# A 27th seven-product unit and one written order for the whole stream: attention and a gated feed-forward block on one core

## The chip, the core and the metric

The kernel runs on one core of a Trainium2 chip. The metric is the device time of one execution in microseconds. Before the change the median of three runs was 404.07 us (403.4 to 404.55).

The core has a matrix engine (TensorE, PE in the profile), whose loads of stationary weights are listed apart (PEld); VectorE (DVE), ScalarE (ACT) and GpSimd (POOL) for elementwise work; and SyncE (SP), which only issues transfers here. POOL issues the loads, SP the transposing transfers and the stores, ACT a few stores at the end. Each engine runs its own instructions in the order in which the program gave them, and waits for the others by semaphores.

## The reference

```python
def _attn_ref(q, k, v):                       # q, k, v: (8, 12, 448, 64)
    scores = scale * np.matmul(q, k.transpose(0, 1, 3, 2))
    attn = np.maximum(scores, 0.0) ** 2 / S
    return np.matmul(attn, v)
...
def _moe_ref(x, w_gate, w_val, w_out):        # x: (3584, 768), d_ff = 1536
    g = x @ w_gate
    gelu = 0.5 * g * (1.0 + erf(g * inv_sqrt2))
    val = x @ w_val
    return gelu * val @ w_out
```

There are eight batches of 12 heads with 448 positions. Attention squares the positive part of the scores in place of a softmax, so no sum over a row is needed. Its output, with the heads side by side, is the input of the feed-forward block.

## The kernel before

**Tiles of the matrix engine.** Nearly every matmul uses one quarter of the array: 64 rows by 64 columns, chosen by a row half and a column half. `mm` (line 364) issues it; this is the line 365 under which nearly all matmuls appear. Two matmuls of the two column halves go out together, and two streams, called PE0 and PE1 in the planner, feed the two row halves side by side.

**Batches.** A batch goes through these steps:
- Loads of q, k and v by POOL (`load_qk`, `load_v`).
- Transposes of q and k: on the matrix engine for batches 0 and 1 (`add_transposes`, an item "t"), by a DVE copy and two transposing transfers on SP's queue for later batches (`add_dma_transposes`, copy at line 475, transfers at line 480).
- 21 scores items (`add_scores`, an item "s"): four matmuls, a relu on ACT (line 714) and a square on DVE (line 728).
- Six values items (`add_values`, "v"), each for a pair of heads, and a scaled copy into `xT` (line 792).
- Gate and value: the 1536 columns of each of the two weights lie in 12 blocks of 128. A plain item (`add_gate_value`) makes one block of gate or of value for a batch with 24 matmuls of 448 columns; a gelu on ACT (line 1044) reads the gate, a multiplication on DVE (line 1049) the value.
- Down products: `add_product`, by groups of four chunks of 64 tokens, seven products of 24 matmuls with 384 columns in place of eight, their sums at line 1143, the results read at lines 1223 and 1225, stored at line 1241.

**Seven-product units.** `add_pair` makes gate and value of two neighbouring blocks at once, as one seven-product scheme of 2 by 2 blocks: the tokens of a batch are cut into two halves of 224 (`halves`), the inner dimension into two halves of 384. Each of the products, named 1 to 7, has 24 matmuls of 224 columns. Three results are copied by ACT (line 962), three are added by DVE (line 966), two gelus (line 970) and two multiplications (line 975) follow. The scheme needs sums of the weights, four for each pair of blocks (`add_pair_sums`, line 870, an item "w"), and sums of the tokens, four for each batch (`add_token_sums`, line 894). `NPB` says how many units a batch has: (0, 1, 2, 3, 4, 4, 6, 6), 26 in all. The other blocks are plain.

**Order.** `LINE` lists gate and value items (a digit is the batch), products of units ("3B6" is batch 3, second unit, product 6) and down products ("d4" is the fourth group, product 4). Before the change, transposes, scores and values are not in `LINE`: lines 1335 to 1376 work out a place for each from the start of the batches in `LINE` and from the twelve numbers of `SHIFT`, and the weight sums are put behind the last plain item of the batch ahead of their first use. `START` is the order of batch 0's attention.

**Planner.** What is placed up to `FIXED` is a fixed list (batch 0's attention, the first transposes of batch 1, the first two plain items). Everything later is a `Unit`. `run_plan` keeps a time for each engine by given costs, and when the matrix engine is free and the fixed list is used up, `next_unit` looks at the first 40 units (`AHEAD`) by rank and takes the first that is ready, or the earliest. Scores may also be put into the midst of another unit. The emitted program is what the planner chose; on the chip each engine's order is then fixed.

**Banks.** The PSUM has two double banks for scores at first. `next_scores` gives one of them up at a point that is called `WIDE` (20.0 on the planner's scale), for two more banks for the feed-forward block; from there each scores item waits for the relu of the one before.

The lines on which the argument rests:

```python
    NPB = (0, 1, 2, 3, 4, 4, 6, 6)
...
        if at > WIDE and n % SB == 0 or wide:
...
    for b, m in late:
        add_dma_transposes(b, m)
```

Of the kernel before, what the change touches and what calls it, by code (L numbers as in the profile page):

```python
# [11 lines left out]
LINE = """  # L12
0 0 0 0 0 0 0 0 0 0 0 0 0 0 0 0 0 0 0 0 0 0 0 0 1 1A1 1 2 1A6 2 2 1 1A7 1A2 1A5 2 a1 2 a2 2A1 1A4 1
1 1 1A3 1 2 1 2A2 a6 1 2A7 a7 2 1 a5 1 1 2A6 2 2 1 1 1 1 a3 1 1 a4 1 1 b1 b7 c1 b2 b6 2A4 2 c6 b4 b5
c7 c5 2B1 2B6 c4 2B2 c3 b3 2A5 2 c2 2B7 2B4 2B5 2A3 2 3A1 2 3A2 2 2B3 2 2 3A6 3A7 d7 d1 3B1 d2 4C1
3B2 3 3C1 3B7 3 d6 3 e1 d4 3C7 3 3C6 3 3B6 e7 3B4 e6 3A4 3A5 3 3 3 3C2 3 3B5 3 3 d5 3C4 3A3 3C5 d3
4A1 4C2 3B3 3C3 e5 3 4A7 f1 f2 f6 e4 f7 4C7 4 e2 4C6 4A2 e3 g7 4B1 f5 4B6 4 4A6 4B2 g1 4B7 4 g2 4A5
4C5 4A4 4B4 4B5 f4 4D7 4D1 4C4 4 5B1 5 4D6 4D5 4A3 4 g6 4 g5 4C3 4B3 f3 4 5 5B2 4D2 4D4 g3 4D3 5C1
g4 5B6 5B7 5C2 5B5 5A1 4 5A6 5 5C7 5A7 5A2 5 5B4 5D1 h1 5A4 5D6 5D2 h6 5C6 h7 5 5D7 5D5 5A5 6A1 5B3
5 5C5 5C4 5A3 5C3 5D4 6B1 5 5D3 5 6A2 6B2 h4 i1 i2 6B7 6A6 i7 h5 6A7 h2 6D1 6F7 6D7 h3 j1 6D6 6C1  # L20
6D2 i6 j7 6E1 j6 6C7 6C2 6E7 i5 i4 6C6 6B6 6A5 6A4 6E6 6A3 6F1 6B4 6B5 6C5 6D5 6D4 6F6 i3 6B3 6F5
6C4 j5 6D3 6E2 6F2 6E5 6F4 6C3 6F3 6E4 6E3 7E7 j2 7E1 7B1 k1 k7 7E2 7A1 7B2 7B7 k2 7B6 7E6 j4 7C1 k6
7A2 l7 7C7 7C6 7A7 7B4 7C2 l1 7B5 7B3 k5 7A6 7F1 j3 7D1 7E5 7F7 7F2 7A5 k4 7F6 7E4 l6 7D7 7C4 7D2
7F4 7D6 7D5 7D4 7D3 l2 7F5 7A4 7C5 7C3 7E3 7A3 l5 l4 7F3 m1 n1 m7 k3 l3 m2 m6 n6 m5 n7 n4 m3 n5 n2
m4 n3
# [7 lines left out]


SHIFT = "-183 -79.5 40.75 1.75 -343.75 -112 43.75 -179.5 27.25 -513.5 -447.25 0.25"
# [60 lines left out]
class Unit:  # L96


    def __init__(self, at, los, his, box=None, closer=None, prev=None):
        self.at, self.los, self.his, self.box, self.closer, self.prev = at, los, his, box, closer, prev  # L100
        self.begun = False
        self.short = False
# [3 lines left out]
BANK = 0.3  # L106


def run_plan(queues, pools, units, banks, arrivals, together, fill, blocks, span):
# [48 lines left out]
    def next_unit(short):  # L158
        best = None
        now = max(free["PE0"], floor)  # L160
        for u in units[:AHEAD]:
# [16 lines left out]
            if u.box is not None:  # L178
                k, end = None, None
                for n, c in banks.items():  # L180
                    x = 0.0 if c is None else c.end
                    if x is not None and (end is None or x < end):
                        k, end = n, x
                if k is None:
                    continue
                t = max(t, end + BANK)
            if short and t > now:
                continue
            t = max(t, now)
            if best is None or t < best[0]:  # L190
                best = (t, u, k)
# [7 lines left out]
    while left:  # L199
# [33 lines left out]
        if isinstance(op, tuple):  # L233
            _, u, k = op
            u.begun = True
            units.remove(u)
            if k is not None:
                u.box["k"] = k
                banks[k] = u.closer()
            queues["PE0"][at["PE0"]:at["PE0"]] = u.los  # L240
# [36 lines left out]
def kernel(  # L277
# [39 lines left out]
    NPB = (0, 1, 2, 3, 4, 4, 6, 6)  # L317
    ROOM = 4
    RING_V, RING_T, RING_H, RING_R, RING_A, RING_O = 3, 3, 2, 2, 4, 4
    SINGLE = "3"  # L320
    RING_M, RING_G = 5, 4
# [17 lines left out]
    loaded = tc.tile_pool(name="lpool", bufs=2), tc.tile_pool(name="hpool", bufs=RING_H)  # L339
# [126 lines left out]
    def add_dma_transposes(b, m, deps=()):  # L466
# [23 lines left out]
        copy = Op("DVE", 0.62, emit_copy, [wait, *(regrouped[n - 2] if n > 1 else ())], lag=0.15, prio=1)  # L490
# [43 lines left out]
    def next_scores(at):  # L534

        n = len(units)
        if at > WIDE and n % SB == 0 or wide:
# [48 lines left out]
    def then(at, step, los, his, box=None, closer=None):  # L586

        if not isinstance(at, list) and at > FIXED:
# [3 lines left out]
            later.append(Unit(at, los, his, box, closer))  # L592
# [567 lines left out]
    def add_product(at, gr, name, final):  # L1160
# [103 lines left out]
        then(at, RS, *ops, box if name in opens else None, lambda: st["read", stages_last[stage]])  # L1264
# [38 lines left out]

    work = []
    flow = [[("g", b, fc, g) for fc in range(2 * NPB[b], FC) for g in range(2)] for b in range(B)]
    line = []
    for x in LINE.split():
        if len(x) == 1:
            line.append(flow[int(x)].pop(0))
        elif len(x) == 3:  # L1310
            line.append(("7", int(x[0]), "ABCDEFGHIJKL".index(x[1]), x[2]))
        else:
            line.append(("p", "abcdefghijklmn".index(x[0]), x[1]))
    assert not any(flow)
    at = 0.0
    starts = [None] * B
    placed = []
    for item in line:
        if item[0] == "g" and starts[item[1]] is None:
            starts[item[1]] = at  # L1320
        if item[0] == "7" and starts[item[1]] is None:
            starts[item[1]] = at
        placed.append((at, item))
        at += {"g": G, "7": G / 2, "p": R}[item[0]]
    starts.append(at)
    WIDE = 20.0
    for at, item in placed:
        if item[0] == "g":
            work.append((at, 5, add_gate_value, item[1:]))
        elif item[0] == "7":  # L1330
            work.append((at, 5, add_pair, item[1:]))
        else:
            _, gr, name = item
            work.append((at, 5, add_product, (gr, name, gr == B * SC // 4 - 1)))
    LEAD = 6.0

    LO1 = 2.0
    for b in range(B):
        if b == 0:
            lo, hi = -60.0, -12.0  # L1340
        elif b == 1:
            lo, hi = LO1, starts[1] - LEAD
# [154 lines left out]
```

## Time and profile before

| | us |
|---|---|
| median of the runs | 404.07 |
| span of the profiled execution, first to last instruction | 394.9 |
| median less that span | 9.2 |
| PE busy | 386.3 |
| DVE busy | 309.6 |
| ACT busy | 258.7 |
| POOL busy | 97.2 |
| mean granted clock of TensorE, share | 0.998 |

The page has the busy time of each engine, the span in slices, the chain of work that ended last, and the costliest groups of instructions, each with its count, its busy time, the mean of one in ns, and the idle time of the engine ahead of it with what ended that. Times of instructions that overlap are counted once in a busy time. The profiled execution's own time is not listed apart from its span.

Further views that are used: a table of stretches (busy time of each engine in a stretch, the number of instructions in brackets, the granted clock, the share of the transfer engines and GB/s), the timeline (start, length, engine, line, operation, and in square brackets the idle time before it with its releaser), and the groups with different shapes kept apart.

### The profile page before, as it was taken

What the parts mean: (1) busy time and instruction counts of PE and PEld (TensorE: products, weight loads), DVE (VectorE), ACT (ScalarE), POOL (GpSimd) and SP (SyncE); (2) the same over time, 40 slices, a digit from 0 to 9 for tenths busy, and PEclk for the clock granted to TensorE, in tenths of its full rate; (3) what the DMA queues carried; (4) which work ended last, traced back from release to release, by engine and by line L of the source; (5) the groups of instructions that cost most, each with busy time, mean ns of one, the idle gap of its engine ahead of it and who ended that gap; (6) DMA issues with size and microseconds to landing.
All of it is one profiled execution on the core that took longest, in us unless ns stands there. A gap on an engine that the chain in (4) does not pass through costs nothing.

```text
span 394.9 us, 22904 instructions
## 1 busy us (share of the span) xinstructions
PE 386.3 (98%) x10570; PEld 358.4 (91%) x10573; DVE 309.6 (78%) x522; ACT 258.7 (66%) x401; POOL 97.2 (25%) x156
## 2 busy tenths in 40 slices
PE   7999999999999999999999999999999999999995
PEld 3458889999999999999999999989999999999994
DVE  3885779968797499999797779758988999866772
ACT  5866872357677767787786478765787886535541
POOL 7656523322233323232332123310211000000000
PEclk9999999999999999999999999999999999999999
DMA  8999999988999969887999598880763501121134
GB/s 110 186 199 199 197 209 185 112 103 83 161 148 175 152 85 143 93 132 121 113 148 108 124 122 111 139 83 11 103 105 56 125 6 43 45 45 45 43 85 120
DMA packets 85567, 45.12 MB, mean 114 GB/s; under 512 B 46048, under 2 KB 82400, under 8 KB 85472
## 3 DMA queue, kind: packets, MB, share of 16 engines
q0 software_dynamic: 46944, 24.39, 49.9%
q1 hardware_dynamic: 37888, 18.49, 26.4%
q8 instruction: 82, 1.34, 1.4%
q10 hardware_dynamic: 640, 0.79, 0.6%
q14 instruction: 13, 0.11, 0.1%
HBM read 48.76 MB, written 11.01 MB: 151 GB/s over the span
## 4 chain that ended last, share of the span: by engine, by line
PE 93%; DVE 2%; DMA 2%; POOL 1%; issue 1%; ACT 0%; ACTq 0%; POOLq 0%
PE ff L365 85%; PE sp L365 7%; DMA qk<-in_k_dram 2%; DVE attnT L728 1%; PE sp L646 1%; POOL qk L424 1%; DVE xT L792 0%; PE ff L646 0%; ACTq L1241 0%; ACT osb L1225 0%; ACT rl L714 0%; PE ff L567 0%; DVE osb L1223 0%; DVE qkT L650 0%; POOL ident masks.py:199 0%
## 5 line engine op out<-in xcount | busy, mean ns | idle before, releaser
L714 ACT ACTIVATE rl<-sp 128x896 bf16<-128x896 f32 x168 | 152.1, 919 | 50.4 <-PE sp L365 45.1
L365 PE MATMUL ff<-xT,wg 64*64 64x224 bf16 (+1 forms) x2304 | 183.7, 299 | 0.6 <-issue 0.6
L365 PEld LDWEIGHTS <-wv 64*64 64x64 bf16 x2304 | 127.7, 107 | 4.4
L365 PEld LDWEIGHTS <-wg 64*64 64x64 bf16 x2304 | 123.3, 107 | 5.0 <-issue 0.5
L365 PE MATMUL ff<-xT,wv 64*64 64x448 bf16 x1056 | 120.8, 349 | 0.0
L728 DVE TENSOR_TENSOR attnT<-rl 128x1792 bf16<-128x1792 bf16 (+1 forms) x98 | 92.2, 952 | 6.6 <-ACT rl L714 6.2
L365 PEld LDWEIGHTS <-ws 64*64 64x64 bf16 x1872 | 92.3, 107 | 1.4 <-issue 1.0
L365 PEld LDWEIGHTS <-s 64*64 64x64 bf16 x1344 | 81.6, 107 | 1.8
L365 PE MATMUL ff<-attnT,v 64*64 64x448 bf16 (+1 forms) x768 | 79.7, 326 | 0.7 <-DVE attnT L728 0.6
L365 PE MATMUL ff<-ts,wv 64*64 64x224 bf16 x1248 | 78.7, 256 | 0.0
L365 PE MATMUL ff<-ts,ws 64*64 64x224 bf16 x1248 | 77.6, 256 | 0.0
L365 PE MATMUL sp<-qkT 64*64 64x448 bf16 (+1 forms) x768 | 74.6, 328 | 0.7 <-issue 0.3
L365 PE MATMUL ff<-wo,s 64*64 64x384 bf16 x672 | 63.4, 323 | 0.0
L966 DVE TENSOR_TENSOR part<-ff,part 128x448 f32<-128x448 f32 x78 | 47.5, 622 | 20.1 <-PE ff L365 16.4
L365 PEld LDWEIGHTS <-uT 64*64 64x64 bf16 x1008 | 62.5, 107 | 0.7
L365 PE MATMUL ff<-wt,s 64*64 64x384 bf16 x672 | 61.4, 322 | 0.0
L365 PE MATMUL ff<-wo,uT 64*64 64x384 bf16 x672 | 60.7, 322 | 0.0
L962 ACT COPY part<-ff 128x448 f32<-128x448 f32 x78 | 41.3, 534 | 12.4 <-PE ff L365 11.2
L443 POOL DMA_DIRECT2D v<-in_v_dram x48 | 29.6, 620 | 80.3 <-ACT rl L714 44.3
L365 PEld LDWEIGHTS <-v 64*64 64x64 bf16 x768 | 44.7, 107 | 4.1 <-issue 1.7
L424 POOL DMA_DIRECT2D qk<-in_q_dram x43 | 27.6, 642 | 80.0 <-ACT rl L714 59.5
L1049 DVE TENSOR_TENSOR uT<-gel,ff 128x448 bf16<-128x448 bf16 x44 | 27.3, 620 | 22.4 <-PE ff L365 11.0
(51 smaller groups left out, 423.9 us busy)
## 6 DMA issues: line engine op xcount, KB each, us to landing
out_dram<-osb SPq DMA_DIRECT2D x48, 192.0 KB, 3.3
v<-in_v_dram POOLq DMA_DIRECT2D x48, 128.0 KB, 4.1
wg<-in_moe_w_gate_dram POOLq DMA_DIRECT2D x6, 384.0 KB, 10.4
wv<-in_moe_w_val_dram POOLq DMA_DIRECT2D x6, 384.0 KB, 11.0
wo<-in_moe_w_out_dram POOLq DMA_DIRECT2D x4, 576.0 KB, 14.9
qk<-in_q_dram POOLq DMA_DIRECT2D x18, 128.0 KB, 3.5
qk<-in_k_dram POOLq DMA_DIRECT2D x18, 128.0 KB, 4.3
qk<-in_q_dram POOLq DMA_DIRECT2D x18, 96.0 KB, 3.8
```

What stands on the lines that cost most here:

```text
L365: ins = nc.tensor.matmul(o, lhsT, rhs, start=start, stop=stop, skip_group_check=onto, tile_position=(P * row, P * col))
L424: return nc.gpsimd.dma_start(qk16[b, m][HALF[i], r0:r0 + h1 - h0, cols], src[b, h0:h1].rearrange("h (p c) d -> p h (c d)", c=SC)[:, :, cols])
L443: return nc.gpsimd.dma_start(v16[b, m][HALF[i], h0 % 4:h0 % 4 + h1 - h0, :, :], v[b, h0:h1].rearrange("h (p c) d -> p h c d", c=SC)[:, :, ...
L646: blocks.add(nc.tensor.transpose(t[HALF[j], c, :], src[:, 2 * r + j, c, :], ident[:, :], tile_position=(0, P * j)))
L714: relu.ins = nc.scalar.activation(duo["rl"][:, u % 2, :, :], box[0][:, :, 0:S], AF.Relu).ins
L728: nc.vector.tensor_tensor(a[:, part], duo["rl"][:, part], duo["rl"][:, part], op=ALU.mult)
L962: rd.ins = nc.scalar.copy(st["t", name][:, :], box[0][:, 0:S]).ins
L966: rd.ins = nc.vector.tensor_tensor(t[:, :], box[0][:, 0:S], t[:, :], op=ALU.add).ins
L1049: u_op[b, fc].ins = nc.vector.tensor_tensor(uT[b][:, fc, :], gel.pop((b, fc))[:, :], box[0][:, 0:S], op=ALU.mult).ins
```

## The change

- `NPB` is (0, 2, 2, 3, 4, 4, 6, 6): batch 1 has two units, 27 in all.
- `LINE` is replaced by one of 566 items that also holds the scores "s", values "v" and transposes "t" of batches 1 to 7, each in its natural sequence, and the weight sums "w0" to "w5". `SHIFT` and the lines that worked out places are gone; an item's place is 1.0 plus its number in `LINE`.
- `WIDE` is now a count: 44 scores and transposes items.
- `Unit` and `run_plan` learn of a unit that takes a second bank (`more`, `full`, `COVER`), and the ring of `lpool` has a name, `RING_L`.
- The pools of loads are also closed at the end when nothing closed them earlier.

```diff
@@ LINE @@
-0 0 0 0 0 0 0 0 0 0 0 0 0 0 0 0 0 0 0 0 0 0 0 0 1 1A1 1 2 1A6 2 2 1 1A7 1A2 1A5 2 a1 2 a2 2A1 1A4 1
...
-7F4 7D6 7D5 7D4 7D3 l2 7F5 7A4 7C5 7C3 7E3 7A3 l5 l4 7F3 m1 n1 m7 k3 l3 m2 m6 n6 m5 n7 n4 m3 n5 n2
-m4 n3
+s s t s s 0 0 0 v 0 s w0 0 0 s s s v s 0 0 0 t s s s s s s s s v s 0 0 0 v v s s s s s s s s s s s s
+s v 1B1 w1 1B7 1A7 s v 1 1 1 1 0 s s 0 0 0 1A1 s 0 1 1 1 s s s s s s 0 0 s s 1B2 v v 1B6 0 a7 1B5
+1B4 s s 1 1 1B3 1A6 1A5 0 a1 1A2 0 a2 1 1A4 a6 1A3 a5 a4 2A1 1 1 v a3 1 v b1 s s s 1 1 s v 2A2 1 b6
...
+7D6 7A5 7F4 7A4 7F3 7D5 7E3 7D4 k4 7B5 7D3 7C5 7C3 7A3 7B4 7B3 l2 m1 m7 l6 k3 m6 m5 l5 l3 n1 n6 n7
+m4 n5 n3 n4 l4 m3 n2 m2
...
-SHIFT = "-183 -79.5 40.75 1.75 -343.75 -112 43.75 -179.5 27.25 -513.5 -447.25 0.25"
...
+            k2 = None
+            if u.more is not None:
+                for n, c in banks.items():
...
+            if k2 is not None:
+                u.more[0]["k"] = k2
+                banks[k2] = u.more[1]()
+                if not full[k2]:
+                    u.more[0]["cover"] = True
+                    u.los[0].cost += COVER
...
-    NPB = (0, 1, 2, 3, 4, 4, 6, 6)
+    NPB = (0, 2, 2, 3, 4, 4, 6, 6)
...
+    RING_L = 2
...
-        if at > WIDE and n % SB == 0 or wide:
+        if n >= WIDE and n % SB == 0 or wide:
...
+    for x in START.split():
+        at = placed0[x.rstrip("a")]
...
+    work.append((PLACE5, add_values, (0, NPAIR - 1)))
+    work.append((PLACE5 + 0.05, add_transposes, (1, 0, (0, 1))))
+    for g in range(2):
+        work.append((0.0, add_gate_value, flow[0].pop(0)[1:]))
+    for n, x in enumerate(LINE.split()):
+        at = 1.0 + n
+        if x[0] == "w":
+            work.append((0.0, lambda at, i: add_pair_sums(i), (int(x[1]),)))
+        elif x == "s":
+            work.append((at, add_scores, flow_s.pop(0)))
...
+    WIDE = 44
...
+    if not rest:
+        for pool in loaded:
+            pool.__exit__(None, None, None)
```

140 lines of the change are left out of this document (53 added, 87 removed).

## The prediction

> **What bounds the kernel now.** I read the page's first part, then its chain of waits, then a table of stretches.
>
> ```profile
> span 394.9 us, 22904 instructions
> PE 386.3 (98%) x10570; PEld 358.4 (91%) x10573; DVE 309.6 (78%) x522; ACT 258.7 (66%) x401; POOL 97.2 (25%) x156
> ...
> PE 93%; DVE 2%; DMA 2%; POOL 1%; issue 1%; ACT 0%; ACTq 0%; POOLq 0%
> ```
>
> ```profile
> 0.00:10.00 10.00, 7.98 (x78) 3.79 (x79) 3.09 (x8) 5.50 (x8) 7.88 (x18) 1.00 0.82 111
> 10.00:20.00 10.00, 9.08 (x140) 4.90 (x142) 8.25 (x15) 8.35 (x11) 6.01 (x9) 1.00 1.36 186
> 20.00:30.00 10.00, 9.14 (x161) 5.35 (x158) 8.75 (x16) 5.85 (x8) 5.40 (x8) 1.00 1.37 199
> 60.00:70.00 10.00, 10.00 (x232) 9.20 (x228) 9.20 (x18) 2.63 (x5) 2.45 (x4) 1.00 1.24 174
> 70.00:80.00 10.00, 10.00 (x277) 9.68 (x271) 9.59 (x18) 3.17 (x7) 3.93 (x6) 1.00 1.10 120
> 260.00:270.00 10.00, 9.35 (x330) 8.98 (x324) 6.33 (x12) 6.27 (x13) 0.61 (x1) 1.00 0.59 45
> 390.00:394.90 4.90, 0.73 (x10) 0.30 (x5) 0.00 (x0) 0.75 (x2) 0.00 (x0) 0.82 0.50 139
> ```
>
> TensorE is the bound: 93% of the chain. The columns after each stretch are its length and the busy time of PE, weight loads, DVE, ACT and POOL. PE is idle for 394.9 - 386.3 = 8.6 us, and these rows hold it all: 2.02, 0.92 and 0.86 in the first 30 us, 0.65 in 260 to 270, 4.17 at the end. So after the first 30 us there is one visible hole. But "busy" is not "at its pace", so I count the work after 30 us and give it its pace.
>
> ```profile
> L365 PE MATMUL ff<-xT,wv 64*64 64x448 bf16 x1046 | 119.7, 349 | 0.0
> L365 PE MATMUL ff<-xT,wg 64*64 64x448 bf16 x1042 | 117.4, 349 | 0.0
> L365 PE MATMUL ff<-ts,wv 64*64 64x224 bf16 x1248 | 78.7, 256 | 0.0
> L365 PE MATMUL ff<-ts,ws 64*64 64x224 bf16 x1248 | 77.6, 256 | 0.0
> L365 PE MATMUL ff<-xT,wg 64*64 64x224 bf16 x1248 | 76.0, 256 | 0.6 <-issue 0.6
> L365 PE MATMUL ff<-attnT,v 64*64 64x448 bf16 x504 | 65.2, 349 | 0.0
> L365 PE MATMUL ff<-wo,s 64*64 64x384 bf16 x672 | 63.4, 323 | 0.0
> L365 PE MATMUL ff<-wt,s 64*64 64x384 bf16 x672 | 61.4, 322 | 0.0
> L365 PE MATMUL ff<-wo,uT 64*64 64x384 bf16 x672 | 60.7, 322 | 0.0
> L365 PE MATMUL sp<-qkT 64*64 64x448 bf16 x504 | 56.9, 349 | 0.0
> L365 PE MATMUL ff<-xT,ws 64*64 64x224 bf16 x624 | 39.6, 256 | 0.0
> L365 PE MATMUL ff<-wt,uT 64*64 64x384 bf16 x336 | 34.1, 323 | 0.0
> L365 PE MATMUL ff<-attnT,v 64*64 64x224 bf16 x168 | 23.5, 256 | 0.0
> L365 PE MATMUL sp<-qkT 64*64 64x224 bf16 x168 | 9.8, 256 | 0.0
> L646 PE MATMUL sp<-ident,qk 128*64 128x128 bf16 x56 | 2.1, 222 | 0.0
> ```
>
> ```profile
> 259.31 0.35 PE L365 MATMUL ff<-xT,wg 64*64 64x448 bf16 x2
> ...
> 260.07 0.35 PE L365 MATMUL ff<-xT,wg 64*64 64x448 bf16 x2
> ...
> 263.10 0.80 PE L365 MATMUL ff<-ts,wv 64*64 64x224 bf16 x24
> 263.68 0.26 PE L365 MATMUL ff<-ts,ws 64*64 64x224 bf16 x2
> ...
> 266.12 0.25 PE L365 MATMUL ff<-xT,wg 64*64 64x224 bf16 x1 [0.65 <-issue]
> ```
>
> ```profile
> 383.30 0.33 PE L365 MATMUL ff<-wt,uT 64*64 64x384 bf16 x2
> ...
> 384.11 0.33 PE L365 MATMUL ff<-wt,uT 64*64 64x384 bf16 x2
> ...
> 388.35 2.38 PE L365 MATMUL ff<-wo,s 64*64 64x384 bf16 x36
> ```
>
> The first block counts matmuls from 30 us on; the others are the timeline of PE. A 64*64 matmul fills a quarter of the array, so its listed duration (349 ns) is latency and the distance between starts is the price. From 259.31 to 260.07 the pairs of one row half advance four times, 0.19 us each, and the other half runs beside it: four 448-column matmuls cost 0.19 us. The 24 matmuls of 224 columns, which are one of the seven products, take 263.68 - 263.10 = 0.58 us. Five steps from 383.30 to 384.11 make 0.162 us for four of 384 columns.
>
> Demand after 30 us: 448 columns, 1046 + 1042 + 504 + 504 = 3096, by four, by 0.19: 147.1. Columns 224: 3 x 1248 + 624 + 168 + 168 = 4704, by 24, by 0.58: 113.7. Columns 384: 3 x 672 + 336 = 2352, by four, by 0.162: 95.3. The transposes 2.1. Together 358.2 us. The last matmul ends at 388.35 + 2.38 = 390.73, so 360.7 us were there: **2.5 us** is all that the order of the work loses after 30 us. (A pace is read to about 0.5%, so this is good to 2 us.) Of it 0.65 is the hole before 266.12. About 0.6 belongs to the end: the last 36 matmuls start over 2.38 - 0.32 = 2.06 us, where their pace would be 36 / 4 x 0.162 = 1.46, since the second row half of a last product runs alone. That stays with any order. So **1.9 us** can be won by order.
>
> **The change part by part.**
>
> The unit. Batch 1 has two blocks of gate and value that took four plain products of 24 matmuls with 448 columns: 4 x 6 x 0.19 = 4.56 us. The second unit takes seven products: 7 x 0.58 = 4.06. It saves **0.50 us**. All of it counts, since PE sets the end.
>
> On the rows above, 24 ns pass for each matmul of 224 columns. [...]
>
> What the unit adds on other engines:
>
> ```profile
> L966 DVE TENSOR_TENSOR part<-ff,part 128x448 f32<-128x448 f32 x78 | 47.5, 622 | 20.1 <-PE ff L365 16.4 <-ACT part L962 3.1
> L962 ACT COPY part<-ff 128x448 f32<-128x448 f32 x78 | 41.3, 534 | 12.4 <-PE ff L365 11.2 <-DVE uT L975 0.3
> L870 DVE TENSOR_TENSOR ws<-ws,wg 128x768 bf16<-128x768 bf16 x6 | 3.3, 552 | 0.0
> L1223 DVE TENSOR_TENSOR osb<-ff,osb 128x384 f32<-128x384 f32 x42 | 23.2, 555 | 8.9 <-PE ff L365 7.5 <-issue 0.5 <-ACT part L962 0.3
> L1225 ACT COPY osb<-ff 128x384 f32<-128x384 f32 x56 | 26.7, 478 | 23.2 <-PE ff L365 22.8
> ```
>
> Three adds of 0.622 on DVE (1.9 us) and three copies of 0.534 on ACT (1.6 us); gelus and multiplications are two and two in both forms. DVE is at 78% and ACT at 66%, so over the whole run they lie beside PE. The four sums of the second weight block (4 x 0.55 = 2.2 us on DVE) were made before too, but now they stand in the list ahead of batch 1's units. That cover is thin from 60 to 80 us, where DVE is at 9.20 and 9.59 of 10; if it is gone, rival D prices it.
>
> The new order. START and what is placed up to FIXED are as before, and later units may start only when that list is used up, about 30 us; so the first 30 us and their 3.8 us of holes stay. I cost them at nothing. From there each item's place in LINE is its rank, and the planner still takes the first ready one of 40, so the list is a preference. It can win at most the 1.9 us, and it can lose: it moves scores, with them the loads that wait for relus, the transposes on SP's queue and the stores behind these. The trace of before can't show where those land. Bounds: -1.9 (every loss gone) and +2.9 (rival D). I take half of what can be won, **-0.95**: the hole at 266.12 is tied to what ran beside it there, and the new list puts other items there, while the thin spread of the rest has no one cause that an order takes away. This is nearer to the lower bound because only one hole is seen in 360 us.
>
> The changed loads, the branch that closes pools, "full", "more" and COVER: no caller gives "more", so no second bank is taken and COVER isn't added. RING_L is the 2 that stood there. WIDE as 44 counts scores and transposes of the first two batches (21 + 21 + 3 = 45), the same place as before within one unit. Nothing for these.
>
> The end. The last item was n3, read by a copy on ACT; now it is m2, read by an add on DVE: 0.555 - 0.478 = **+0.08 us**. The store after it goes by the same two queues.
>
> Sum: -0.50 - 0.95 + 0.08 = -1.4 us. The profiled execution's span is 394.9, so the new span is 393.5; outside it lie 404.07 - 394.9 = 9.2 us to the median of the runs, which I carry over. **Forecast 402.7 us**, -0.34%.
>
> **The rivals.**
>
> B, the order wins all: -0.50 - 1.9 + 0.08 gives 401.7, and with the 2 us of doubt in the pace 399.7 at the far end. For it: scores were placed by a few shifts for each batch and can now stand anywhere. Against: the 1.9 us is spread thin.
>
> C, the order wins nothing: only the unit and the end, 403.6 us. For it: the planner deviates from the list whenever an item isn't ready, in both kernels, so the executed orders may differ little in quality.
>
> D, slower: DVE becomes the bound between 60 and 80 us. Sums of the second weight block (2.2 us) and the three adds (1.9) move in where 0.80 + 0.41 = 1.2 us is free: DVE is 2.9 us late, the products of batch 1 wait for its sums, the first down products after them, and PE with all of them. 404.07 - 0.42 + 2.9 = 406.6 us. It decides as soon as DVE is asked for more than 10 us in 10 while no ready plain unit is left. Against it: ten of batch 0's gate and value units stand behind the second block's sums in the new list and need nothing from them.
>
> E, slower: holes of "issue" like the one at 266.12 multiply.
>
> ```profile
> q8 instruction: 82, 1.34, 1.4%
> DMA to landing us min/median/max: 2.7/4.6/7.2
> ```
>
> The first row counts the packets that bring instructions: 1.34 MB in 82, 16.3 KB each, for 10570 + 10573 PE instructions, or 258 in one. In a stretch of 224-column products one lasts 129 x 24 ns = 3.1 us. The second is the landing time of the 36 transposing transfers (qkT from qkr), 4.6 us: longer than a block lasts, so a block that comes in behind one can be late. The new unit adds 7 x 24 - 4 x 24 = 72 matmuls and as many loads. If the new order puts three more transfers beside such stretches: 3 x 0.65 = +1.95, and 404.07 - 0.42 + 1.95 = 405.6 us. Against it: in 360 us with 36 such transfers it shows once.
>
> [...] That the hole at 266.12 is a late block is my reading; no row names it.
>
> **How the numbers follow.** From no change this kernel can be told at about 0.3%, 1.2 us: faster is below 402.86, slower above 405.28. The forecast has 0.44, and its own range, 401.8 to 403.6, goes over the lower bound: 0.29 faster, 0.15 same. B has 0.17, all faster. C has 0.12, of it 0.02 faster by the doubt in the pace and 0.10 same. D has 0.14 and E 0.13, slower both but for 0.02 of E that stays within the bound. So 0.48 faster, 0.27 same, 0.25 slower. The range goes from B's far end, 399.7, to D's 406.6, and leaves out D's upper half and what is worse.
>
> **What would show it.** Right: 7 x 26 + 7 = 189 products of 24 matmuls, PE busy past 98%, the last matmul some 1.4 us before 390.7; no PE idle above 0.3 us after 30 us. The unit's step is wrong if starts within a seven product are more than 0.58 us apart. D shows as PE idle, or matmuls below pace, between 50 and 100 us with DVE as the releaser; E as "issue" holes beside transposing transfers. The forecast as a whole is wrong if the first 30 us differ, or if scores starve: the relu (L714) then waits longer for PE and the values come late.

## The result: slower by 0.7%, and the profile after

| | before | after |
|---|---|---|
| median of 19 runs each, us | 400.74 (396.91 to 404.55) | 403.13 (399.49 to 406.25) |
| ratio, 95% interval | 1 | 1.007 (1.0047 to 1.0092) |
| time of the profiled execution, us | not listed | 404.35 |
| its span, us | 394.9 | 402.6 |

The ratios, here and below, leave out the few slow runs, so they differ a little from the quotients of the medians.

The forecast was 402.7 us, faster by 0.34%. The change is slower. That 403.13 lies near 402.7 is no merit: the base has moved, since the three runs of 404.07 that the prediction started from stand at the upper end of the 19.

The first parts of the page of after:

```profile
span 402.6 us, 23039 instructions
PE 389.4 (97%) x10642; PEld 356.8 (89%) x10645; DVE 312.0 (78%) x525; ACT 262.9 (65%) x404; POOL 96.5 (24%) x156
...
q8 instruction: 83, 1.36, 1.4%
...
PE 91%; DMA 3%; DVE 2%; issue 2%; ACT 1%; ACTq 0%; POOL 0%; POOLq 0%
```

TensorE is still the bound, and the 72 more matmuls of the second unit are there (10642 - 10570). But PE is now idle for 402.6 - 389.4 = 13.2 us where it was idle for 8.6, and it is busy for 3.1 us more although the unit asks for 0.5 us less. The first number is holes; what the second is comes below. Where the holes are shows in the stretches of 10 us of after (columns as before: length, busy time of PE, weight loads, DVE, ACT, POOL, then clock, share of the transfer engines, GB/s):

```profile
0.00:10.00 10.00, 8.31 (x77) 3.99 (x78) 2.71 (x7) 5.00 (x7) 7.38 (x17) 1.00 0.78 104
10.00:20.00 10.00, 9.63 (x147) 5.14 (x147) 8.70 (x16) 8.93 (x12) 6.53 (x10) 1.00 1.37 191
20.00:30.00 10.00, 9.13 (x156) 5.14 (x156) 8.58 (x16) 5.69 (x7) 6.05 (x10) 1.00 1.37 199
60.00:70.00 10.00, 9.00 (x234) 8.02 (x229) 8.05 (x14) 2.70 (x6) 2.45 (x4) 1.00 1.25 177
130.00:140.00 10.00, 8.51 (x245) 7.71 (x240) 6.51 (x10) 6.65 (x11) 2.61 (x4) 1.00 1.16 192
140.00:150.00 10.00, 8.82 (x243) 8.42 (x235) 6.43 (x10) 6.56 (x10) 2.45 (x4) 1.00 0.56 71
260.00:270.00 10.00, 9.74 (x338) 9.43 (x330) 8.55 (x15) 7.82 (x13) 2.34 (x4) 1.00 0.50 61
```

The first 30 us have 2.93 us of idle PE (3.80 before). From 60 to 70, where before had none, 1.00 us is lost, from 130 to 150 it is 2.67. The hole of before, at 266, is smaller. The table of what PE waited for after 28 us, first before, then after (us in total, times, the longest):

```profile
PE ff L365 <- issue: 0.6, 1, 0.6
```

```profile
PE ff L386 <- issue: 5.0, 11, 1.2
PE sp L386 <- DMA qkT<-qkr: 0.7, 1, 0.7
PE sp L386 <- issue: 0.2, 1, 0.2
```

L386 is the line that was 365. **"Issue" means that PE waited for nothing that the profile shows**: no engine, no bank, no transfer of data. One such hole became twelve, 5.2 us together. Six of them in the timeline of PE (start, length, and in brackets the idle time ahead):

```profile
58.18 0.38 PE L386 MATMUL ff<-xT,wv 64*64 64x448 bf16 x2 [0.16 <-issue]
64.10 0.38 PE L386 MATMUL ff<-xT,wg 64*64 64x448 bf16 x2 [0.37 <-issue]
69.47 0.28 PE L386 MATMUL ff<-ts,ws 64*64 64x224 bf16 x2 [0.62 <-issue]
...
132.10 0.25 PE L386 MATMUL ff<-ts,ws 64*64 64x224 bf16 x1 [0.35 <-issue]
...
138.12 0.28 PE L386 MATMUL ff<-attnT,v 64*64 64x224 bf16 x1 [1.14 <-issue]
...
143.49 0.28 PE L386 MATMUL ff<-ts,wv 64*64 64x224 bf16 x2 [1.18 <-issue]
```

The listed idle time is less than what a hole costs, since it counts from the end of the last matmul, 0.26 to 0.35 us behind its start. From the last start ahead of a hole to the first behind it the twelve come to 8.7 us (0.50 at 58.18, where 0.16 is listed). So the holes also account for most of the busy time that was gained: the other 3.5 us lie under PE's busy time.

And the stretches of after from the end of one hole to the end of the next:

```profile
58.18:64.10 5.92, 5.55 (x128) 4.80 (x128) 4.45 (x8) 2.48 (x5) 1.22 (x2) 1.00 1.23 205
64.10:69.47 5.37, 4.75 (x128) 4.27 (x128) 4.45 (x9) 1.61 (x3) 1.83 (x3) 1.00 1.36 173
132.10:138.12 6.02, 4.88 (x128) 4.30 (x128) 3.68 (x6) 4.48 (x7) 1.72 (x3) 1.00 1.27 212
138.12:143.49 5.37, 4.19 (x128) 3.87 (x128) 4.22 (x7) 2.37 (x3) 1.50 (x3) 1.00 0.93 135
```

This is the reading on which most of what follows rests. Between two neighbouring holes stand exactly 128 matmuls and 128 weight loads, 256 instructions, in each of the four. A packet of instructions holds 1.36 MB / 83 = 16.4 KB, and there are (10642 + 10645) / 83 = 256 matmuls and weight loads for each. So the holes look like late instruction blocks, and the time from one to the next, 5.4 to 6.0 us here, is how long a block took to come.

No row of the page names them so, but the trace has the start and the length of each packet of the instruction queue, q8. The views of the transfers show them too: from 58.18 to 61.80 us there is no packet of q8, and from 61.80 to 62.80 there is this one, whose 6.1% of 16 engines' time in 1 us are 0.97 us:

```profile
q8 instruction: 1, 0.02, 6.1%
```

| hole before ended, us | packet starts | lasts | landed | next hole ends | from landing to that |
|---|---|---|---|---|---|
| 58.18 | 61.82 | 0.97 | 62.79 | 64.10 | 1.31 |
| 64.10 | 67.23 | 0.96 | 68.19 | 69.47 | 1.28 |
| 132.10 | 135.73 | 0.94 | 136.67 | 138.12 | 1.45 |
| 138.12 | 141.09 | 0.97 | 142.06 | 143.49 | 1.43 |

The same holds in all the profiled executions of this document, 20 of them: each of their 84 "issue" holes between 30 and 386 us ends at the same place in its execution's count of 256, within one instruction, and 1.2 to 1.7 us behind the landing of a packet. And in none of the 1611 blocks of these traces does the first instruction start sooner than 1.2 us behind a landing (1.27 in before, 1.22 in after). **So the holes are late instruction blocks.** What is late is the packet's start: it lasts 1.0 us in the median, but starts up to 4.2 us behind the border at which the block ahead of its own begins to run (below, "its border"). In none of them does it start more than 0.3 us before that border (0.24 in before).

128 matmuls of 224 columns are used up in 128 x 24 ns = 3.1 us, 128 of 448 columns in 32 x 0.19 = 6.1 us. From hole to hole above it takes 5.4 to 6.0 us: a block of wide matmuls lasts that long, a block of narrow ones doesn't.

In before the late blocks cost PE 0.6 us of "issue" in 395 us, in after 5.2 us in 403.

### The profile page after: what moved, and what is told of

It is laid out like the page before. It is cut to its first block, busy times and chain, and to the rows that moved or that the text cites. A ratio compares the mean times of both kernels' runs of the same rounds, so it can differ in the third digit from the quotient of the medians.

```text
span 402.6 us, 23039 instructions
## 1 busy us (share of the span) xinstructions
PE 389.4 (97%) x10642; PEld 356.8 (89%) x10645; DVE 312.0 (78%) x525; ACT 262.9 (65%) x404; POOL 96.5 (24%) x156
## 3 DMA queue, kind: packets, MB, share of 16 engines
q8 instruction: 83, 1.36, 1.4%
## 4 chain that ended last, share of the span: by engine, by line
PE 91%; DMA 3%; DVE 2%; issue 2%; ACT 1%; ACTq 0%; POOL 0%; POOLq 0%
PE ff L386 81%; PE sp L386 8%; DMA qkT<-qkr 2%; DVE attnT L749 1%; ACT rl L735 1%; DMA qk<-in_k_dram 1%; PE sp L667 1%; DVE xT L813 0%; PE ff L667 0%; PE ff L588 0%; ACTq L1262 0%; PE ff L630 0%; ACT osb L1246 0%; DVE osb L1244 0%; DVE qkT L671 0%
## 5 line engine op out<-in xcount | busy, mean ns | idle before, releaser
L735 ACT ACTIVATE rl<-sp 128x896 bf16<-128x896 f32 x168 | 151.9, 921 | 51.6 <-PE sp L386 48.0
L386 PE MATMUL ff<-xT,wg 64*64 64x224 bf16 (+1 forms) x2304 | 177.3, 297 | 0.4 <-issue 0.4
L386 PEld LDWEIGHTS <-wv 64*64 64x64 bf16 x2304 | 124.2, 107 | 6.7 <-issue 3.4
L386 PEld LDWEIGHTS <-wg 64*64 64x64 bf16 x2304 | 122.3, 107 | 4.8 <-issue 1.1
L386 PE MATMUL ff<-xT,wv 64*64 64x448 bf16 x1008 | 116.2, 349 | 0.2 <-issue 0.2
L386 PEld LDWEIGHTS <-ws 64*64 64x64 bf16 x1944 | 99.6, 107 | 3.5 <-issue 2.7
L386 PE MATMUL ff<-ts,ws 64*64 64x224 bf16 x1296 | 83.6, 256 | 1.5 <-issue 1.5
L386 PE MATMUL ff<-attnT,v 64*64 64x448 bf16 (+1 forms) x768 | 81.7, 326 | 1.8 <-issue 1.1
L386 PEld LDWEIGHTS <-s 64*64 64x64 bf16 x1344 | 80.3, 107 | 3.2 <-issue 0.4
L386 PE MATMUL ff<-ts,wv 64*64 64x224 bf16 x1296 | 80.7, 256 | 1.2 <-issue 1.2
L386 PE MATMUL sp<-qkT 64*64 64x448 bf16 (+1 forms) x768 | 77.6, 328 | 1.4 <-DMA qkT<-qkr 0.7
L386 PE MATMUL ff<-wo,s 64*64 64x384 bf16 x672 | 64.2, 323 | 0.0
L386 PE MATMUL ff<-wt,s 64*64 64x384 bf16 x672 | 63.9, 323 | 0.3 <-issue 0.3
L386 PEld LDWEIGHTS <-uT 64*64 64x64 bf16 x1008 | 61.8, 107 | 1.4
L386 PE MATMUL ff<-wo,uT 64*64 64x384 bf16 x672 | 62.9, 323 | 0.0
L386 PEld LDWEIGHTS <-v 64*64 64x64 bf16 x768 | 45.4, 107 | 5.3 <-issue 3.1
L1246 ACT COPY osb<-ff 128x384 f32<-128x384 f32 x56 | 26.9, 481 | 29.5 <-PE ff L386 29.0
```

The lines of the kernel that those rows point to most:

```text
L386: ins = nc.tensor.matmul(o, lhsT, rhs, start=start, stop=stop, skip_group_check=onto, tile_position=(P * row, P * col))
L735: relu.ins = nc.scalar.activation(duo["rl"][:, u % 2, :, :], box[0][:, :, 0:S], AF.Relu).ins
L1246: ins = nc.scalar.copy(o, box[0][:, 0:OGS])
```

## The experiments

All ratios are to the kernel before, in runs on the same chip. "Idle" is the idle time of PE in a stage, its length less PE's busy time, in one profiled execution. These are the stages of before, of after, and of after profiled once more:

```profile
30.00:60.00 30.00, 30.00 (x653) 25.20 (x648) 19.92 (x27) 22.19 (x30) 14.17 (x20) 1.00 1.35 202
60.00:75.00 15.00, 15.00 (x377) 14.17 (x373) 13.84 (x26) 4.75 (x9) 6.35 (x10) 1.00 1.08 150
75.00:340.00 265.00, 264.35 (x7575) 255.57 (x7569) 221.97 (x369) 188.94 (x293) 57.40 (x93) 1.00 0.76 106
340.00:386.00 46.00, 46.00 (x1537) 45.62 (x1532) 31.79 (x63) 22.17 (x44) 0.00 (x0) 1.00 0.24 56
```

```profile
30.00:60.00 30.00, 29.84 (x665) 24.64 (x663) 24.18 (x36) 22.87 (x31) 13.51 (x19) 1.00 1.36 202
60.00:75.00 15.00, 14.00 (x374) 12.95 (x369) 12.03 (x21) 3.77 (x7) 5.61 (x10) 1.00 1.01 145
75.00:340.00 265.00, 260.63 (x7414) 249.78 (x7409) 215.94 (x354) 190.49 (x291) 57.45 (x93) 1.00 0.80 106
340.00:386.00 46.00, 45.67 (x1572) 44.41 (x1565) 33.28 (x62) 22.77 (x44) 0.00 (x0) 1.00 0.18 43
```

```profile
30.00:60.00 30.00, 29.65 (x651) 24.20 (x647) 24.32 (x37) 22.45 (x31) 14.24 (x21) 1.00 1.36 201
60.00:75.00 15.00, 13.73 (x374) 12.72 (x368) 11.25 (x21) 4.16 (x8) 5.43 (x10) 1.00 1.03 151
75.00:340.00 265.00, 263.74 (x7551) 254.85 (x7547) 219.83 (x361) 191.63 (x294) 58.03 (x94) 1.00 0.79 107
340.00:386.00 46.00, 44.89 (x1503) 42.87 (x1496) 31.94 (x63) 22.10 (x44) 0.00 (x0) 1.00 0.20 47
```

All the kernels in one table; "plain" says that the transposing transfers are plain copies:

| kernel | ratio (95%) | idle 30 to 60 | 60 to 75 | 75 to 340 | 340 to 386 |
|---|---|---|---|---|---|
| before | 1 | 0 | 0 | 0.65 | 0 |
| before, repeat (e14) | 0.9998 (0.9966 to 1.003) | 0 | 0 | 1.09 | 0 |
| before, repeat (e15) | 0.9985 (0.9954 to 1.0015) | 0 | 0.46 | 1.14 | 0 |
| after | 1.007 (1.0047 to 1.0092) | 0.16 | 1.00 | 4.37 | 0.33 |
| after, repeat (e16) | 1.004 (1.0008 to 1.0072) | 0.35 | 1.27 | 1.26 | 1.11 |
| order alone (e1) | 1.0056 (1.002 to 1.0091) | 0 | 0.74 | 2.46 | 0.27 |
| unit alone (e2) | 1.0093 (1.0059 to 1.0127) | 0 | 0.46 | 2.79 | 0.33 |
| after, plain (e3) | 1.0008 (0.9973 to 1.0043) | 0.32 | 1.27 | 0.67 | 1.23 |
| before, plain (e4) | 0.9938 (0.9897 to 0.998) | 0 | 0.46 | 0 | 0.09 |
| before, plain, repeat (e5) | 0.9951 (0.9907 to 0.9996) | 0 | 0 | 0.51 | 0 |
| after, plain, wide items late (e6) | 0.9956 (0.9928 to 0.9984) | 0 | 0 | 0.90 | 0.04 |
| after, plain, end mixed (e7) | 0.9988 (0.9956 to 1.002) | 0.47 | 1.54 | 1.54 | 0.32 |
| after, later marks (e8) | 1.0063 (1.0028 to 1.0098) | 0.17 | 0.72 | 3.90 | 0.05 |
| after, wide items late (e10) | 1.0049 (1.0021 to 1.0077) | 0 | 1.41 | 1.42 | 0.39 |

### Which half of the change costs the time

Order alone (e1): after with 26 units. The seven products of unit 1B become four plain items and w1 moves behind them.

```diff
-    NPB = (0, 2, 2, 3, 4, 4, 6, 6)
+    NPB = (0, 1, 2, 3, 4, 4, 6, 6)
```

> The changed kernel with the second unit of batch 1 taken back (four plain products in its place, so 26 units): the new order alone. Theory L (blocks of 256 PE instructions arrive late, behind transfers that the new order puts beside them; the order is the cause): 1 to 4 us slower than before, several holes of 0.3 to 1.4 us in the PE row that wait for nothing but issue. Theory U (the extra unit, its DVE and ACT work, is the cause): within 0.5 us of before or faster. If only the unit's saving is lost, it is 0.5 us slower than the changed kernel.

Unit alone (e2): before with a second unit in batch 1; its products take the places of four "1" in the old list.

```diff
-    NPB = (0, 1, 2, 3, 4, 4, 6, 6)
+    NPB = (0, 2, 2, 3, 4, 4, 6, 6)
@@ LINE @@
-... 1 1 1A3 1 2 1 2A2 ... 2 1 1 1 1 a3 1 1 a4 ...
+... 1 1B1 1B2 1 1A3 1 2 1 2A2 ... 2 1 1B6 1B7 1 1 a3 1B5 1B4 1B3 a4 ...
```

> The kernel before with a second unit of batch 1 put into its own order in place of four plain products: the unit alone, the old way of placing scores and values. Theory U: about 2 us slower than before. Theory L: the unit is worth its 0.5 us, and what comes on top depends on whether the plan that follows puts transfers beside block boundaries: between 0.5 us faster and 2 us slower, with the sum of the issue holes after 30 us explaining the difference to before within 1 us.

Measured: 403.34 us for the order alone, ratio 1.0056, which can't be told from the whole change at 1.007. **The order alone is enough for the loss**, 3.47 us of idle PE against 0.65. The unit's 0.50 us, the difference between e1 and after, is below what these runs resolve. The unit in the old list costs 0.93%, more than either theory allowed: it too makes holes (3.58 us idle, of them 1.1 a wait for a transposing transfer). That everything behind its four places lies otherwise against the block borders is the likely reason, but wasn't tested apart.

### Are the transposing transfers the cause?

Rival E named them as what makes a block late. In both kernels each is replaced by a plain copy of the same bytes, so that q and k of batches 2 to 7 aren't transposed.

```diff
-            ins = nc.sync.dma_start_transpose(
-                qkT_tile(b, m)[:, c0:c1].rearrange("d c r x -> d (c r) x"),
+            ins = nc.sync.dma_start(
+                qkT_tile(b, m)[:, c0:c1].rearrange("d c r x -> d (c r x)"),
```

> The changed kernel with each transposing transfer from qkr to qkT replaced by a plain copy of as many bytes at the same place, so q and k of batches 2 to 7 aren't transposed and their scores are of other pairs. Theory L: the holes between 100 and 300 us go (from some 6 us in the profiled run of the changed kernel to under 1.5 us), and the time is 2 to 6 us under the changed kernel's 403.1. Theory O (the new order starves PE by DVE, ACT or banks, and the transfers don't matter): within 1 us of 403.1, holes as before.

> The kernel before with the same replacement (q and k of batches 2 to 7 not transposed). Theory L: it gains less than the changed kernel, 0 to 3 us, and the two with plain copies lie within 1 us of each other, the changed one ahead by the unit's 0.5 us. Theory O: the changed one stays 2 to 3 us behind.

Measured: 400.86 us for after and 397.79 for before. Either kernel is 0.3 to 0.6% faster without the transposing. From 75 to 340 us the idle time falls to 0.67 and to 0, but after's repeat with the transposing has 1.26 there and a later plain kernel (e7) 1.54, so a single execution proves little. The packets say the same more surely, and that it is a small effect: from 75 to 300 us a packet starts 0.84 us behind its border in the median of the five plain executions and 1.05 in the fifteen others. **The gap between the two kernels stays**, 3.1 us. So the transposing transfers aren't what separates them, and E's cause falls where its mechanism stands. What is left in e3 sits in other places: 1.27 us from 60 to 75 and 1.23 from 340 to 386. Its last part from hole to hole:

```profile
353.49:357.78 4.29, 3.91 (x129) 3.66 (x129) 2.58 (x5) 2.02 (x4) 0.00 (x0) 1.00 0.37 96
357.78:361.80 4.02, 3.98 (x129) 3.59 (x130) 1.51 (x3) 2.60 (x5) 0.00 (x0) 1.00 0.40 102
361.80:365.82 4.02, 3.75 (x129) 3.49 (x130) 2.50 (x5) 1.36 (x3) 0.00 (x0) 1.00 0.02 4
365.82:369.84 4.02, 3.72 (x130) 3.47 (x130) 2.69 (x6) 1.68 (x4) 0.00 (x0) 1.00 0.02 4
```

The same count again, a block within two or three instructions, and 4.02 us for one with only 4 GB/s beside it, against 5.4 to 6.0 beside 135 to 212 GB/s. Before at the same place:

```profile
350.20:360.20 10.00, 10.00 (x372) 9.94 (x365) 5.62 (x11) 5.30 (x11) 0.00 (x0) 1.00 0.36 84
```

737 instructions in 10 us without a hole, a block in 3.5 us. So 4.0 us isn't a fixed time of delivery. The packets show the difference: in e3's last three blocks here they start 1.11 to 1.57 us behind the border and last 0.88 to 1.44, in before from 350 to 360 they start 0.56 to 1.08 behind it and last 0.96 to 1.01. Why a packet starts later in one execution than in another, with hardly any traffic beside it, stays open.

### Is it narrow code where the loads run?

Four kernels followed. Before, plain, with a register move after every fourth matmul (e5) was to make the blocks shorter in matmuls:

```diff
+        seen[0] += 1
+        if seen[0] % 4 == 0:
+            nc.tensor.reg_mov(n_reg, 0)
```

> The kernel before with plain copies (q and k of batches 2 to 7 not transposed), and after every fourth matmul one register move on PE's queue that nothing uses: 1/8 more PE instructions, no more work on the array. Theory L (a block of 256 instructions can't come in under about 3.5 us, whatever the array does): a block of 224-column code is used up in 2.7 us in place of 3.1, so there is a hole at nearly each block boundary in dense stretches, and the time goes up by 10 us or more over the kernel with plain copies alone (397.8), while the pace inside a block stays 0.19 us for four matmuls of 448 columns. Rival P (an instruction costs PE's queue its own time): the pace of 448-column code rises too, everywhere alike, and no holes at the boundaries. If instructions don't matter, 397 to 399.

The moves weren't in the program that ran, which has 22904 instructions and 82 packets of them, as before. So it is a second measurement of e4, 0.9951 beside 0.9938, and its question stays open.

After, plain, with eight of batch 0's wide plain items ahead of unit 1B (e6):

```diff
-s v 1B1 w1 1B7 1A7 s v 1 1 1 1 0 s s 0 0 0 1A1 s 0 1 1 1 s s s s s s 0 0 s s 1B2 v v 1B6 0 a7 1B5
+s v 0 0 0 0 0 0 0 0 1B1 w1 1B7 1A7 s v 1 1 1 1 s s 1A1 s 1 1 1 s s s s s s s s 1B2 v v 1B6 a7 1B5
```

> The changed kernel with plain copies (q and k of batches 2 to 7 not transposed) and eight plain gate and value items of batch 0 moved ahead of batch 1's units: wide matmuls, whose blocks last 6 us, stand in the stretch of 55 to 70 us where the loads fill the transfer engines. Theory L: the holes at 58, 64 and 70 us (2.3 us in the kernel with plain copies alone) go to under 1 us, the time 1 to 1.5 us under 400.9. Rival: they wait for the loads themselves or for DVE, and stay within 0.5 us.

After, plain, with k4, l6, k3, l5 and l3 spread among batch 7's products (e7):

```diff
-... 7A7 7A2 7D1 7F1 7C4 7F2 7F6 7D2 7F7 ... 7B6 7F5 7D6 ... k4 7B5 ... l6 k3 m6 m5 l5 l3 n1 ...
+... 7A7 7A2 7D1 7F1 k4 7C4 7F2 7F6 7D2 l6 7F7 ... 7B6 7F5 k3 7D6 ... l5 7F3 ... 7B5 l3 ... m6 m5 n1 ...
```

> The changed kernel with plain copies (q and k of batches 2 to 7 not transposed) and five down products moved from the end of LINE into the row of 24 products of units of batch 7, one after each four or five. Theory L: the holes of 340 to 381 us, with no load left in that stretch, come from 224-column code that uses up its blocks faster than they come; mixed with 384-column products they drop from 3.3 us to under 1.5 us, the time 1 to 2 us under 400.9. Rival: the end then lacks cover for its last sums and loses it again, within 0.5 us.

After with the planner's marks of block borders, behind which it puts the transposing transfers, 56 instructions later (e8):

```diff
-    blocks = Blocks(256, 256 - 192 + 10, 36, (110, 4))
+    blocks = Blocks(256, 256 - 192 + 10, -20, (110, 4))
```

> The changed kernel, whole, with the transposing transfers tied to a PE instruction 20 past a block boundary in place of 36 ahead of it (28 matmuls later): each starts behind the fetch of the next block in place of ahead of it. Theory L: holes beside transfers between 100 and 300 us fall from some 6 us to under 3, the time is 1 to 3 us under 403.1. Rival: the transfer then runs into the fetch after, and nothing is won: 402.5 to 404.5.

**e6 is the one that answers.** 398.78 us, 0.9956, level with before's plain form (0.9938 and 0.9951) and 1.5 us under e7 on the same chip; its interval just overlaps that of e3, which ran on another. The stretches from 50 to 60 us show why: first before, then after, then e6.

```profile
50.00:55.00 5.00, 5.00 (x114) 3.97 (x109) 3.80 (x6) 3.89 (x5) 1.46 (x3) 1.00 1.24 210
55.00:60.00 5.00, 5.00 (x111) 4.28 (x107) 3.38 (x6) 3.51 (x5) 1.22 (x2) 1.00 1.16 210
```

```profile
50.00:55.00 5.00, 5.00 (x123) 4.56 (x116) 4.45 (x8) 4.39 (x7) 1.22 (x2) 1.00 1.24 207
55.00:60.00 5.00, 4.84 (x123) 4.08 (x119) 4.56 (x7) 4.10 (x6) 1.22 (x2) 1.00 1.16 211
```

```profile
50.00:55.00 5.00, 5.00 (x116) 4.31 (x111) 4.43 (x8) 4.50 (x6) 1.23 (x3) 1.00 1.25 209
55.00:60.00 5.00, 5.00 (x114) 4.31 (x110) 4.77 (x8) 3.51 (x5) 1.22 (x2) 1.00 1.17 212
```

Here the loads move 210 GB/s, among the most of the run. Before uses 225 + 216 = 441 PE instructions in these 10 us, a block in 5.8 us; after 246 + 235 = 481, a block in 5.3; e6 451, a block in 5.7. Blocks come in 5.4 to 5.9 us at 58 to 69 us. The old order keeps just within that and the new one doesn't. The packets bear it out: the three behind the borders from 46 to 59 us start 3.62 to 3.82 us late in before, 3.37 to 3.64 in after and 3.55 to 3.75 in e6. So beside the loads the blocks are late in either order, and only the code that waits for them differs. With eight wide items there the holes at 58, 64 and 69 us are gone: idle from 30 to 75 us falls from 1.59 us (e3) to 0.

e7 takes the idle time at the end from 1.23 to 0.32, but its 0.9988 can't be told from e3. e6 has 0.04 there with the end untouched, so the holes at the end come and go by themselves; after and its repeat (0.33 and 1.11) say the same. e8, at 1.0063, changes nothing that can be measured: where the transfers are put beside the borders by 56 instructions isn't the lever.

### Mending the whole kernel

After with e6's move and the transposing transfers left as they are (e10):

> The changed kernel, whole, with eight plain gate and value items of batch 0 moved ahead of batch 1's units, as with the plain copies. Theory L: the 1.2 to 1.9 us of holes between 58 and 70 us go and the ones between 100 and 300 us beside transposing transfers stay: 1 to 2 us under the changed kernel, ratio to before 0.999 to 1.005. Rival: another plan draws another set of collisions and the time stays at 1.005 to 1.01 of before.

e10 with each transfer cut into three pieces (e11):

```diff
-                          ... enumerate(((0, VC), (VC, SC)))]
+                          ... enumerate(((0, 3), (3, 5), (5, 7)))]
```

> The same, with the two transposing transfers of each third of a batch (4 and 3 columns) cut into three (3, 2 and 2), each held back by the planner until a block boundary is near. Theory L: a block waits behind a shorter transfer, so the delivery of a block between two neighbouring holes falls from 5.4 to 6.0 us to about 5, and the holes from 100 to 300 us to under half: 1 to 2 us under the kernel with late units. Rival: there are 54 transfers in place of 36, each with its own fixed cost, and the time stays or rises by up to 2 us.

The planner puts a transposing transfer behind a mark near a block border, and only if it counts on its end within `BLOCK` from that mark; `GATE_T` is the time that it counts for one. e10 with a shorter `BLOCK` (e12), and after with twice the `GATE_T` (e13):

```diff
-    GATE_T, BLOCK = 1.2, 7.1
+    GATE_T, BLOCK = 1.2, 4.5
@@ e13 @@
-    GATE_T, BLOCK = 1.2, 7.1
+    GATE_T, BLOCK = 2.4, 7.1
```

> The kernel with late units, where the planner lets a transposing transfer start only when it is through 4.5 us after the boundary mark in place of 7.1 (a dense block lasts 3.1 to 3.8 us). Theory L: fewer of them run into the next fetch, holes from 100 to 300 us under half, 1 to 2 us under the kernel with late units. Rival: the transfers come later, scores wait for them, and the time is the same or up to 3 us more.

> The changed kernel, where the planner reckons a transposing transfer's traffic at 2.4 us in place of 1.2, so that it starts fewer of them late in a block. Theory L: 1 to 2 us under the changed kernel, ratio to before 1.000 to 1.005, with fewer holes from 100 to 300 us. Rival: no difference, 1.005 to 1.01.

Measured: e10 400.67 us, 1.0049 (1.0021 to 1.0077), between after and no change and not to be told from after. The holes at 58 and 64 us are gone, and in their place stands one of 1.40 us at 71, where e6 had none:

```profile
71.00 0.38 PE L382 MATMUL ff<-xT,wg 64*64 64x448 bf16 x2 [1.40 <-issue]
```

So in the whole kernel that repair isn't shown to work. The other three are far worse: e11 424.56 us, 1.0628 (1.0579 to 1.0678); e12 415.98, 1.0433 (1.0389 to 1.0476); e13 414.77, 1.0385 (1.0342 to 1.0428). From 75 to 340 us in e13:

```profile
75.00:340.00 265.00, 261.46 (x7124) 246.35 (x7119) 209.47 (x345) 182.35 (x279) 58.54 (x95) 0.99 0.78 106
```

And from its waits of PE, where the relu of the scores (L735) has come up as a releaser, which it was not in after:

```profile
PE sp L386 <- ACT rl L735: 1.4, 2, 1.0
```

Its idle time in the stage is 3.54 us, less than after's 4.37, but it gets 290 matmuls less done (7124 against 7414), 213 of them from 120 to 140 us (284 against 497). Later transfers bring later scores, and PE then runs below its pace. That is the starving of scores that the prediction named as what would make the forecast as a whole wrong; here, not in the change itself, it came. These three kernels cost 4 to 6%. In two of them the granted clock falls in the same stretch, to 0.68 from 130 to 140 us in e13 and to 0.78 in e12, while e11 keeps 1.00; how much of their loss is the clock's isn't shown.

### Is the old order only a lucky draw?

If the old order were a favourable draw against the block borders, exchanging two neighbours in it should cost as much as the new order. The same rounds measured after again (e16) without any edit.

```diff
@@ e14 @@
-... b4 b5 ...
+... b5 b4 ...
@@ e15 @@
-... d7 d1 ...
+... d1 d7 ...
```

> The kernel before with two neighbouring down products changed over in LINE (b4 b5 to b5 b4, some 110 us in): the same work, the plan differs from there on. Theory D (a draw: the order of before happens to put few transfers at its dense block boundaries, and nearly any other order has 2 to 4 us more of holes): slower than before by 0.3 to 1%, with holes on issue at places where before has none. Theory N (the new list is worse in itself, by its early units and its end): within 0.3% of before.

> The kernel before with another two neighbours changed over (d7 d1 to d1 d7, some 170 us in). Theory D: slower by 0.2 to 1%, all of it from holes after 165 us. Theory N: within 0.3%.

> The changed kernel unaltered, for a second profile and a time beside the two swaps. Both theories: 1.005 to 1.009 of before. Theory L: holes at the same instruction counts as in its first profile, above all 58 to 70 and 132 to 144 us, sized differently by what the transfers did in that execution.

Both swaps left the emitted program as it was, since the planner takes the first item that is ready. So e14 and e15 repeat before: 0.9998 and 0.9985, which shows what a repeat does by itself. The repeat of after gave 402.79 us, 1.004 (1.0008 to 1.0072). Three swaps that change the program followed:

```diff
@@ e17 @@
-... 3A2 2 2B3 2 2 ...
+... 3A2 2B3 2 2 2 ...
@@ e18 @@
-... f7 4C7 4 e2 ...
+... f7 4 4C7 e2 ...
@@ e19 @@
-... 4C4 4 5B1 5 ...
+... 4C4 5B1 4 5 ...
```

> The kernel before with two neighbours changed over in LINE (2 2B3 to 2B3 2); unlike the first two swaps this one changes the program, from instruction 6578 of PE's 21148 on, some 130 us in. Theory D (the old order is a favourable draw): 0.3 to 1% slower than before, by holes on issue at places where before has none, and nothing different ahead of 125 us. Theory N (the new list is worse in itself): within 0.3%.

> The same with another pair (4C7 4 to 4 4C7); the program differs from instruction 10026 on, some 190 us in. Theory D: 0.2 to 0.8% slower, all of it behind 185 us. Theory N: within 0.3%.

> The same with a third pair (4 5B1 to 5B1 4); the program differs from instruction 11666 on, some 215 us in. Theory D: 0.2 to 0.7% slower, all of it behind 210 us. Theory N: within 0.3%.

Measured: e17 401.11 us, 1.0028 (0.9997 to 1.0059); e18 406.86, 1.0184 (1.0105 to 1.0263); e19 406.58, 1.0165 (1.0108 to 1.0223). So one exchange of neighbours can cost more than twice what the whole new order costs: in that sense the old order is a selected one. But the loss in e18 isn't the expected kind. Its "issue" holes after 30 us are few (1.8 us in 3). The stretch ahead of the end, first of before, then of e18:

```profile
320.00:340.00 20.00, 20.00 (x710) 19.86 (x704) 18.82 (x34) 12.79 (x23) 0.00 (x0) 1.00 0.11 25
```

```profile
320.00:340.00 20.00, 19.69 (x581) 17.81 (x573) 16.16 (x27) 12.71 (x21) 0.00 (x0) 1.00 0.09 24
```

PE is hardly idle and yet does 129 matmuls less: it runs below its pace, and that work is left for the end. The timeline of e18 shows how, in part:

```profile
327.47 1.17 PE L365 MATMUL ff<-wt,uT 64*64 64x384 bf16 x12
328.48 0.38 PE L365 MATMUL sp<-qkT 64*64 64x448 bf16 x4
328.91 0.76 PE L365 MATMUL ff<-ts,wv 64*64 64x224 bf16 x12
329.88 0.38 PE L365 MATMUL sp<-qkT 64*64 64x448 bf16 x4 [0.20 <-ACT rl L714]
```

Twelve matmuls of 384 columns, 0.49 us at four in 0.162, take 1.0 us until the next start: one stream runs with no second one beside it, and the scores behind it wait for the relu. So late blocks don't explain every order, and a PE that is 98% busy can still lose 2%.

## Why the prediction was wrong, point by point

**What bounds the kernel**: right, PE in both. **The loss that order can win back**: read as 2.5 us from one execution. It was a low one: its span of 394.9 us is the lowest of three profiled executions of that program (396.4 and 396.6 in the repeats), and their idle times after 30 us are 0.65, 1.09 and 1.60.

**The unit, -0.50**: not contradicted and not shown. e1 and after differ by less than their intervals. **The end, +0.08**: the last group of matmuls in after, below, ends at 395.81 + 2.38 = 398.19, and 4.4 us of the span follow it; before it was 4.2. Small, as said.

```profile
395.81 2.38 PE L386 MATMUL ff<-wo,s 64*64 64x384 bf16 x36
```

**The first 30 us, nothing**: right. 2.93 us of idle PE against 3.80, and no loss there.

**The order, -0.95: this is the step that failed, in sign and in size.** It took half of 1.9 us as won, "because only one hole is seen in 360 us". From 30 to 386 us PE is idle for 5.86 and 3.99 us in the two executions of after, 4.9 in the mean, against 1.1 in the mean of three of before: +3.8 us. Some 3.1 us of that are blocks that come late, 0.5 a wait for a transposing transfer near 109 us. The medians show +2.4; the profiled executions lie further apart (spans of 402.6 and 401.0 against 394.9, 396.4 and 396.6) than the medians do. With the unit's 0.50 taken as earned and the end's 0.08 as lost, the term is some +2.8 by the medians in place of -0.95. The argument was wrong in kind: that the old order showed one hole said something of the old order, not of orders. The prediction's own upper bound (+2.9) just held it, but by another path: that bound was DVE's. The row that should have decided was the one quoted under rival E.

**What lies outside the span, 9.2 us**: wrong. In the profiled execution of after it is 404.35 - 402.6 = 1.75 us, and it is 1.7 to 4.0 in the other runs on record. The rest of the 9.2 was the distance between a low execution and three high runs, and the forecast carried it as if it were fixed.

**Rival D**: didn't come. From 60 to 70 us DVE is at 8.05, lower than before (9.20), and no hole there names it. **Rival E**: its mechanism was right, late blocks of instructions in narrow code, and its size not far off (+1.95 against the order's +2.8). Its cause was only partly right. It counted transposing transfers beside narrow code. The traces show what makes a hole: narrow matmuls use a block up in 3.1 us, and a block's packet starts late, lasts about 1 us, and is of use only 1.2 us or more after it landed. Beside the loads it starts 3.6 us behind its border (the median of 80 from 40 to 62 us), from 300 to 386 us 0.8 (of 441). The part that repeats in every profiled execution with the new order is the one beside the loads: 0.74 to 2.01 us from 30 to 75 in six of them (after, e16, e1, e3, e7, e8), 0 to 0.46 in five executions of the old order. Between 75 and 386 us the holes are late blocks too, but which blocks are late differs from execution to execution; with plain copies and the wide items moved the gap can no longer be measured, with the transposing transfers it isn't shown to shrink. What holds one packet back and not another, away from the loads, wasn't found.

No kernel here beat the one before; only plain forms, which leave the transposing out, are faster (e4, e5 and e6).

## What to carry to other kernels

Where TensorE is the bound and its matmuls are narrow, count instructions along with columns: compare, stretch by stretch, how long 256 of them last (3.1 to 6.1 us here) with how long a block takes to come (4.0 to 6.0 us from hole to hole here), and put wide matmuls where the loads are heaviest (some 210 GB/s here; in e6 that took the holes of that stretch away, in e10 one was left). When PE waits for "issue", count the instructions between two holes; if it is 256 every time, as here, look for the instruction packets in the trace and not for data. And take the base from several executions: a profiled one may lie 1% below the median, and a term carried over from their difference is then as large as the change itself.

## What the runs showed of the hardware beyond that

Packets of instructions start later beside the loads: at some 200 GB/s, from 40 to 62 us, one of 16 KB starts 3.6 us behind its border in the median, from 75 to 300 us 1.05 (0.84 with plain copies) and from 300 to 386 us 0.8. It lasts about 1 us in all three (0.97, 1.08 and 0.96 in after). Plain copies in place of the transposing transfers gain 0.5 to 0.6% in the old order (0.9938 and 0.9951), and in the profiled execution of before TensorE doesn't wait for their data after 30 us. And the runs of one program lie up to 1.9% apart (396.91 to 404.55 us). The granted clock doesn't explain it: of two runs of before on one chip, 397.94 us had 0.997 and 403.62 us had 0.999.
